# Backward pass of sliding-window attention: visits of four key blocks instead of steps of three, with the key-side slabs kept over two chunks

## The chip, the core and the metric

The kernel runs on one core of a Trainium2 chip. The metric is the device time of one execution in microseconds (us); less is better. Engines are named as in the profile: PE (TensorE matmul), PEld (its weight load), DVE (VectorE), ACT (ScalarE), POOL (GpSimd) and SP (SyncE, whose queue issues every DMA here; the profile calls the queue SPq). Each engine runs its own instructions in the order in which the kernel lists them.

## The reference

Four layers in a row, linear attention (A) and sliding-window softmax attention (B) in turn, each with a layer norm before and a residual around, and the gradients of the whole for a given output gradient. S = 2048 rows, D = 640, H = 32 heads of Dh = 20, window W = 256.

```python
def _B_ref(x, wqkv, wo):
    qkv = ((x @ wqkv).reshape(B, S, 3, H, Dh)).transpose(2, 0, 3, 1, 4)
    scores = einsum("bhqd,bhkd->bhqk", q, k) * (Dh ** -0.5)
    mask = (i - j >= 0) & (i - j < W)
    p = softmax(where(mask, scores, -1e9))
    o = einsum("bhqk,bhkd->bhqd", p, v)
    return o.transpose(0, 2, 1, 3).reshape(B, S, D) @ wo
x = x + A(layernorm(x));  x = x + B(layernorm(x))
x = x + A(layernorm(x));  x = x + B(layernorm(x))
out, vjp = jax.vjp(f, A_x, A_wqkv, A_wo, B_wqkv, B_wo);  grads = vjp(grad_out)
```

The change concerns the backward pass of the two B layers (layers 3 and 1), and the form in which the forward pass stores q, k and v for them.

## The kernel before

The execution has five parts in a row: the forward pass (to about 655 us of the span), the attention backward of layer 3 (its first score exponentials start at 654.7 us), the linear backward of layer 2, the attention backward of layer 1 (from 1255.2 us), and the linear backward of layer 0 with the products for the weight gradients.

The attention backward (`core`, L1191) cuts the 2048 rows into 16 query blocks of 128. A **chunk** is two query blocks, so there are 8 chunks for each layer. A query block sees up to three key blocks: its own, the one before and the one before that. Heads go in 8 groups g of four, and a head takes 32 rows of the PE array. One **step** (`core_steps`, L627) is one query block, one pair p of a group's heads, and its three key blocks: 2 heads x 3 blocks, 768 columns. That is 32 steps a chunk: 8 groups x 2 query blocks x 2 pairs.

`core_step` (L655) is a software pipeline written out by hand, with a fixed order on each engine. In step n:

- PE computes `dp` for step n-3 (two matmuls of 384 columns on 32 rows each) and then the scores `s` for step n (two more, on the other 64 rows). Both go to PSUM tiles of which there is only one each (`pS`, `pD`, two banks each).
- ACT takes the exponential, `e` (L677). DVE multiplies, `ds = dp * e` for step n-3 (L680). POOL masks two blocks of `e` (L689, L693).
- The transposed product `dsT` is needed as well. For 13 of 32 steps (the list `bd` of PLACES, used from the third chunk on) a DMA transposes it, issued on SP right after `ds`. For the other steps PE transposes step n-4 into a PSUM tile `flip` (L700), after some idle transposes that keep PE's clock up (`warm`, L173, numbers in `thin`), and ACT (L705) or DVE (L707) copies it out; `on_act` says which, by a count of both engines' loads.
- Then comes a "piece": work of other stages that is put into the step's slot by a list of places (`bf` for `plan_before`, which makes the next chunk's output gradients; `bh` for `plan_behind`, which takes an earlier chunk's dq, dk, dv through the projection, the layer norm and the next product).
- Last, `core_acc` (L713) sums dk, dv and dq of step n-7 (`lag` = 7) with 18 matmuls of 20 columns into two PSUM banks. After each group's four steps ACT and DVE take the sums out (L753 or L755, L757, L759).

The tags "flip" and "dense" share two PSUM banks (`ps2`). A quarter of a chunk (two groups, 8 steps) has one set of slabs: q, k, v transposed (`qT`, `kT`, `vT`) and q, k plain (`qs`, `ks`). `core_loads` (L1176) loads all five at once, one quarter ahead, with k and v for the four key blocks that the chunk sees; three sets are in use by turns. In the forward pass `qkv` (L493) stores q, k, v plain (`sv["s"]`, with v) and transposed (`sv["T"]`), one DMA each for a block of 128 rows.

Chunk 0 sees fewer key blocks (256 or 512 columns a step). Chunks 0 and 1 use no DMA transposes and have no work of `plan_behind`. Chunks 2 to 7 are called steady below.

Of the kernel before, what the change touches and what calls it, by code (L numbers as in the profile page):

```python
# [15 lines left out]
P = 128  # L16
# [30 lines left out]
    bf=[2.1, 3.1, 5.2, 14.9, 17.9, 6.2, 7.8, 10, 14.6, 28.3],  # L47
    bh=[13.1, 14.5, 15.5, 17.1, 17.5, 18, 20, 21.2, 25.7, 28.3, 30, 36, 19.1, 20.1, 21.8, 22.5, 23.3, 24.6, 25.2, 27.5, 30.5, 31.7, 33, 35, 41.5, 43, 2.2, 8.3, 9.5, 12, 18.9, 34.5],
    l2=[-10.4, -1.3, 0.6, 1.2, 1.9, 3.2, 4.6, 6.2, 7, 7.5, 5, 8, 8.3, 10.2, 11.8, 14, 14.4, 15.4, 16, 16.2, 18.7, -2.3, 4.4],
    n1=[9.7, 0.5, 3.3, 3.6, 5.3, 9, 3, 4.7, 5.4, 5.6, 24],  # L50
    xx=[1, 1, 0, 0, 0, 0, 1, 1, 0, 0, 0, 0, 0, 1, 0, 0, 1, 0, 0, 0, 0, 0, 0, 1, 0, 0, 1, 0, 0, 0, 1, 0],
    bd=[0, 0, 1, 0, 0, 0, 1, 0, 0, 0, 0, 0, 0, 1, 1, 0, 0, 1, 1, 0, 1, 0, 1, 0, 1, 0, 1, 1, 0, 1, 1, 0])


class Kern:
    def __init__(self, ctx, tc, x0, A_w, A_wo, B_w, B_wo, grad, outs):
# [27 lines left out]
        for l in (1, 3):  # L84
            self.sv[l] = {k: d(f"{k}{l}", [TT, P, 3, G * P]) for k in ("s", "T")}
# [20 lines left out]
    def dma(self, out, in_, transpose=False):  # L106
        with self.nc.allow_non_contiguous_dma(reason="tiled layouts"):
            return self.nc.sync.dma_start(out=out, in_=in_, transpose=transpose)  # L108

# [129 lines left out]
    def forward(self, st):  # L239
# [28 lines left out]
        st.ring, st.va, st.turn = [], [], 0  # L268
# [32 lines left out]
        def scores():  # L301
# [6 lines left out]
                 (B1 - 1, scores), (c3, lambda: self.close_outer(self.mz[2])),  # L308
# [27 lines left out]
        def before(a):  # L336
            if a == 0:
                first_.update(enumerate(self.slots(self.plan_before(st, 3, 0, st.core, ((1, 2, 3, 8, 10), (2, 4, 5, 10, 12))), 16)))
            if first_[a] is not None:
                first_[a]()  # L340
# [18 lines left out]
    def plan_scores(self, st, l, t, X):  # L359
# [37 lines left out]
        def values(g):  # L397
            self.b_pv(st, l, t, g, [home[g, i] for i in range(nb)], nb, [ring(k0 + i) for i in range(nb)], X[t]["ob"])
# [11 lines left out]
    def plan_ln(self, st, l, t, x, src, key, pool):  # L410
# [3 lines left out]
        def stats(c):  # L414
            if c == 0:
                x["bst"] = st.sm.tile([P, 2, 6], F32, name="bst")
            nc.vector.bn_stats(x["bst"][:, c, :], x[src][:, c * CW:(c + 1) * CW])

        def norm():
            mv = st.sm.tile([P, 2], F32, name="bmv")  # L420
# [13 lines left out]
    def plan_front(self, st, la, lb, t, x, x_in, Wo, W, Wq=None):  # L434
# [24 lines left out]
        def num(c):  # L459
            if c == 0:  # L460
                x["o"] = st.fb.tile([P, D], BF, name="o", bufs=2)
# [12 lines left out]
        def flip_o():  # L474
            self.dma(self.rows(self.o[la], t), x["o"])
# [17 lines left out]
        def qkv(j, c):  # L493
            ps = self.dense(st, x["hnT"], W, j * D + c * CW)
            dst = R["s"][:, j, c * HALF:(c + 1) * HALF, 0:DH]
            src = self.heads(ps[:, 0:CW])
# [6 lines left out]
            if (j, c) == (1, 1):  # L503
                self.dma(R["T"][:, 0:2].rearrange("p a g q -> p (a g) q"), R["s"][:, 0:2].rearrange("p a h d -> p (a h d)"), transpose=True)
            if (j, c) == (2, 1):
                self.dma(sv["s"][t], R["s"].rearrange("p a h d -> p a (h d)"))
                self.dma(R["T"][:, 2], R["s"][:, 2].rearrange("p h d -> p (h d)"), transpose=True)
                self.dma(sv["T"][t], R["T"].rearrange("p a g q -> p a (g q)"))
# [14 lines left out]
    def plan_rear(self, st, l, t, x, x_out, Wo, W):  # L523
# [3 lines left out]
        def flip_o():  # L527
            x["obT"] = self.flip(st.ps, st.fa, x["ob"], "obT", P, DT, P, nc.vector)
# [49 lines left out]
    def plan_feat(self, st, l, t, x, src, W):  # L578
# [8 lines left out]
        def feat_(nm, c, split=False):  # L587
            ps = self.dense(st, x["h2T"], W, {"pq": 0, "pk": D, "v": 2 * D}[nm] + c * CW)
            if nm == "v":
                vt = st.va[t % len(st.va)]  # L590
                nc.scalar.copy(vt[:, c * HALF:(c + 1) * HALF, 0:DH], self.heads(ps[:, 0:CW]))
# [7 lines left out]
            def close():  # L599
                part()  # L600
                if nm == "pk" and c == 1 and l == 2:
# [10 lines left out]
        def outer(c=None):  # L612
            a, b = x["pqk"][:, 1, :], st.va[t % len(st.va)].rearrange("p h d -> p (h d)")
            if c is None:
                if "og" not in x:
                    x["og"] = self.acc_outer(st, [(a, b)], t == 0)
                next(x["og"])
# [9 lines left out]
    def core_steps(self, st, l, S, c, qr, dq):  # L627
# [3 lines left out]
        for g in range(2 * qr, 2 * qr + 2):  # L631
            for bi in range(2):
                b = t0 + bi
                k0 = max(b - 2, 0)
                for p in range(2):
                    class U:
                        pass
                    u = U()
                    u.c, u.g, u.gi, u.b, u.bi, u.p, u.S, u.dq, u.t0, u.w0 = c, g, g - 2 * qr, b, bi, p, S, dq, t0, w0
                    u.nb = b - k0 + 1  # L640
                    u.kk = k0 - w0
                    u.cw = u.nb * P
                    u.by_dma = self.by_dma(32 * c + 4 * g + 2 * bi + p)
                    yield u

    @staticmethod
    def by_dma(n):

        return n >= 64 and PLACES["bd"][n % 32] == 1

    WARM = (6, 4)
    TAIL = 5
    FULL = 3600

    def core_step(self, st, l, u, piece, on_act, thin):  # L655
# [7 lines left out]
        d, f, a = back(3), back(4), back(st.lag)  # L663
        if d is not None:
            d.dp = st.pD.tile([P, 2, 512], F32, name="dp")
            for j in range(2):
                r0 = HP * (2 * d.p + j)
                self.mm(d.dp[:, j, 0:d.cw].rearrange("p (a b) -> p a b", a=d.nb), d.S["dT"][d.bi][r0:r0 + HP, d.g, :],
                        d.S["vT"][r0:r0 + HP, d.kk:d.kk + d.nb, d.gi, :], True, True, (r0, 0))
        if u is not None:  # L670
            s = st.pS.tile([P, 2, 512], F32, name="s")
            for j in range(2):
                r0 = HP * (2 * u.p + j)
# [786 lines left out]
```

## Time and profile before

| | |
|---|---|
| three runs | 2200.07, 2201.24, 2201.99 us; median 2201.24 |
| the profiled execution: its time, its span | 2199.58 us, 2197.9 us; granted PE clock 0.984 |
| DVE, ACT, POOL busy, share of the span | 63%, 61%, 49% |
| DMA moved | 453.26 MB, 81.2% of 16 engines' span |
| first exponential of layer 3's chunks 0 to 7 | 654.7, 699.3, 751.6, 807.1, 865.0, 920.6, 975.6, 1033.3 us |
| first exponential of layer 1's chunks 0 to 7 | 1255.2, 1297.5, 1349.8, 1404.7, 1460.9, 1516.8, 1571.8, 1629.9 us |
| slab loads, KB each (x count) | qT 128 (x64), kT 256 (x56), vT 256 (x56), qs 128 (x64), ks 256 (x56) |
| forward stores of q, k, v, KB each (x count) | plain 768 (x32), transposed 768 (x32) |

Differences of neighbouring entries in the two rows of first exponentials give the time of a chunk: 44.6, 52.3, 55.4, 57.9, 55.7, 54.9 and 57.7 us for layer 3's first seven. A view by window gives, for such a stretch, the busy time of each engine with its number of instructions. A view of the waits lists who waited for whom, with the sum, the number and the longest. "PE busy" counts a stretch in which matmuls are in flight; their ends are modelled.

### The profile page before, as it was taken

Reading aid. Unit: us, or ns where it says so; the run is one execution under the profiler, and the core shown is the slowest. Engines: PE = TensorE matmul, PEld = TensorE weight load, DVE = VectorE, ACT = ScalarE, POOL = GpSimd, SP = SyncE. Lnnn points to the kernel's source line nnn. Section 1 sums busy time; section 2 is a strip of 40 time slices with the busy share of each in tenths; the row PEclk is TensorE's granted clock in tenths of the full one; section 3 lists DMA queues with packets and bytes.
Section 4 is the critical chain, followed back from the end, with each engine's and each line's share of the span. In section 5 each row is a group of like instructions: output and inputs, shape, how many; then the busy total and the mean of one; then the engine's idle time right before and its main releaser. Section 6 shows DMA issues by size and latency. Waiting matters only on the chain. (4 is left out here: it accounts for less than half of the span.)

```text
span 2197.9 us, 74336 instructions
## 1 busy us (share of the span) xinstructions
PE 2041.3 (93%) x30981; PEld 1586.3 (72%) x30981; DVE 1390.2 (63%) x2840; ACT 1342.4 (61%) x2009; POOL 1083.0 (49%) x1887
## 2 busy tenths in 40 slices
PE   7989998899989999998879899999988899999999
PEld 5667776577767877777768687777776788888644
DVE  6788886888836887887748668888876233320000
ACT  5468886388876887887637677888876233330000
POOL 2046665166675577777534456777764312220000
PEclk9999999999999999999999999999999999999999
DMA  7498885799979499998799734999987999998650
GB/s 258 146 253 229 237 233 146 171 234 245 232 218 255 111 200 198 210 206 192 157 293 275 198 106 115 197 208 202 210 189 165 271 307 246 266 228 241 220 162 21
DMA packets 708193, 453.26 MB, mean 206 GB/s; under 512 B 419728, under 2 KB 684688, under 8 KB 707472
## 3 DMA queue, kind: packets, MB, share of 16 engines
q1 hardware_dynamic: 707856, 448.51, 81.2%
q8 instruction: 242, 3.96, 0.8%
q14 instruction: 95, 0.78, 0.1%
HBM read 213.09 MB, written 149.82 MB: 165 GB/s over the span
## 5 line engine op out<-in xcount | busy, mean ns | idle before, releaser
L680 DVE TENSOR_TENSOR ds<-dp,e 128x768 bf16<-128x768 f32 (+2 forms) x512 | 464.0, 906 | 173.8 <-PE s L138 55.6
L677 ACT ACTIVATE e<-s 128x768 bf16<-128x768 f32 (+2 forms) x512 | 395.7, 773 | 137.5 <-PE s L138 110.4
L383 ACT ACTIVATE eT<-sT 128x2048 bf16<-128x2048 f32 x180 | 338.0, 1878 | 89.0 <-PE sT L138 85.2
L138 PE MATMUL wg<-rhs,lhs 128*128 128x240 bf16 (+3 forms) x2880 | 372.2, 286 | 7.7 <-DMA lhs<-o 7.7
L138 PEld LDWEIGHTS <-lhs 128*128 128x128 bf16 x2880 | 262.1, 98 | 97.2 <-DMA lhs<-o 9.6
L689 POOL TENSOR_SCALAR_AFFINE_SELECT e<-e 128x256 bf16<-128x256 bf16 x512 | 207.2, 406 | 249.8 <-ACT e L677 246.9
L138 PEld LDWEIGHTS <-dqT 128*128 128x128 bf16 x1920 | 171.8, 98 | 62.2 <-issue 10.4
L391 POOL TENSOR_SCALAR_AFFINE_SELECT eT<-eT 128x512 bf16<-128x512 bf16 x256 | 165.5, 650 | 98.7 <-ACT eT L383 98.7
L138 PE MATMUL acc<-slabqs,ds 128*128 128x20 bf16 x2880 | 210.0, 172 | 1.4 <-ACT dq L759 0.5
L138 PE MATMUL dp<-slabvT,dT 32*128 32x384 bf16 (+2 forms) x1024 | 168.0, 320 | 44.3 <-DVE ds L680 39.6
L138 PE MATMUL acc<-ds,e 128*128 128x20 bf16 x2880 | 208.0, 171 | 0.0
L138 PEld LDWEIGHTS <-ds 128*128 128x128 bf16 x2880 | 187.9, 96 | 11.7 <-issue 3.5
L693 POOL TENSOR_SCALAR_AFFINE_SELECT e<-e 128x256 bf16<-128x256 bf16 x448 | 194.9, 435 | 0.0
L138 PEld LDWEIGHTS <-e 128*128 128x128 bf16 x2880 | 170.0, 96 | 10.6 <-issue 1.8
L1140 DVE CAST wr<-wg 128x240 bf16<-128x240 f32 (+3 forms) x54 | 24.4, 452 | 240.1 <-PE wg L138 228.8
L700 PE MATMUL flip<-ident,ds 128*128 128x128 bf16 x1944 | 169.7, 221 | 3.3 <-DVE ds L787 1.2
L138 PE MATMUL s<-slabkT,slabqT 32*128 32x384 bf16 (+2 forms) x1024 | 167.9, 323 | 4.1 <-ACT e L677 3.5
L1138 ACT CAST wr<-wg 128x240 bf16<-128x240 f32 (+3 forms) x36 | 14.3, 397 | 245.9 <-PE wg L138 241.3
L1033 POOL TENSOR_TENSOR dh<-dh,lg 128x640 f32<-128x640 f32 x32 | 46.0, 1437 | 238.1 <-DVE s L1030 235.1
L138 PE MATMUL dense<-WTA,dqT 128*128 128x320 bf16 x960 | 162.6, 301 | 0.6 <-DVE dqT L1007 0.3
L138 PE MATMUL dense<-WB,hnT 128*128 128x320 bf16 x960 | 160.1, 301 | 0.4 <-DVE s L500 0.3
L138 PE MATMUL acc<-slabks,dsT 128*128 128x20 bf16 x2880 | 147.3, 171 | 14.0 <-DMA dsT<-ds 13.0
(175 smaller groups left out, 4483.0 us busy)
## 6 DMA issues: line engine op xcount, KB each, us to landing
s<-s SPq DMA_DIRECT2D x32, 768.0 KB, 4.1
T<-T SPq DMA_DIRECT2D x32, 768.0 KB, 3.9
dqkv<-dq SPq DMA_DIRECT2D x16, 960.0 KB, 5.6
dqkv<-dqa SPq DMA_DIRECT2D x32, 480.0 KB, 5.1
rhs<-dqkv SPq DMA_DIRECT2D x32, 480.0 KB, 5.4
rhs<-dqkv SPq DMA_DIRECT2D x16, 960.0 KB, 6.5
slabkT<-T SPq DMA_DIRECT2D x56, 256.0 KB, 4.4
slabvT<-T SPq DMA_DIRECT2D x56, 256.0 KB, 3.9
```

The costliest lines, as they stand in the source:

```text
L138: return self.nc.tensor.matmul(out, lhsT=lhsT, rhs=rhs, start=start, stop=stop, skip_group_check=True, **kw)
L383: nc.scalar.activation(e, s, ACT.Exp)
L391: nc.gpsimd.affine_select(out=e, in_=e, compare_op=ALU.is_ge, fill=0.0, base=0, pattern=[[0, 4], [1, P]], channel_multiplier=-1)
L677: nc.scalar.activation(u.e[:, :, 0:u.cw], s[:, :, 0:u.cw], ACT.Exp)
L680: nc.vector.tensor_tensor(out=d.ds[:, :, 0:d.cw], in0=d.dp[:, :, 0:d.cw], in1=d.e[:, :, 0:d.cw], op=ALU.mult)
L689: nc.gpsimd.affine_select(out=dg, in_=dg, compare_op=ALU.is_ge, fill=0.0, base=0, pattern=[[0, 2], [-1, P]], channel_multiplier=1)
L693: nc.gpsimd.affine_select(out=fr, in_=fr, compare_op=ALU.is_ge, fill=0.0, base=-1, pattern=[[0, 2], [1, P]], channel_multiplier=-1)
L700: nc.tensor.transpose(ps[:, 3 * j + i, :], f.ds[:, j, i * P:(i + 1) * P], self.ident)
L1033: nc.gpsimd.tensor_tensor(out=x["dh"], in0=x["dh"], in1=L["g"][:, i, :], op=ALU.add)
L1138: nc.scalar.copy(o[:, 0:w], ps[:, 0:w])
L1140: nc.vector.tensor_copy(o[:, 0:w], ps[:, 0:w])
```

## The change

The unit of the pipeline becomes a **visit**: four (query block, key block) pairs times two heads, 1024 columns, two full banks. A quarter's two groups have 12 such block pairs for each head pair; they are cut into three visits, so a chunk has 24 visits instead of 32 steps. The same blocks are computed. A visit's blocks are not all of one query block: `s` and `dp` of a visit are issued as "runs" of neighbouring key blocks of one query block (three, two and three runs for the three visits), those of `dp` and of `s` in turn. `lag` is 6 visits. `dsT` has eight blocks; 11 of 24 visits have it transposed by DMA (`bd`). Which engine copies a `flip` and how many idle transposes go before it now comes from fixed lists (`xx`, `th`), in place of the counts. A visit has two places for pieces, before and after `core_acc`; `bf` and `bh` have new numbers, in units of a 32nd of a chunk as before. The sums are taken out after every three visits, for a head pair of two groups, with DVE's add in two halves. Masks at two places of a visit go in one POOL instruction of 512 columns.

The stored transposed q, k, v get a layout with the quarter outside, written by three DMAs in pieces of 512 bytes a row; v is no longer stored plain. A quarter's load is now one DMA for k and v transposed of the chunk's own two blocks, and one for q transposed; the plain k and q are loaded by two more, issued in the second visit of the quarter itself. The blocks of the chunk before are taken from its slabs, which are kept (seven `slabT`, six `slabks`). `B.sf` has one buffer instead of two. The rest are assertions, which issue nothing.

```diff
-    bf=[2.1, 3.1, 5.2, 14.9, 17.9, 6.2, 7.8, 10, 14.6, 28.3],
+    bf=[3, 4.5, 7.7, 8.8, 17.9, 7.2, 9.7, 10, 13.9, 28.1],
...
-    xx=[1, 1, 0, 0, 0, 0, 1, 1, 0, 0, 0, 0, 0, 1, 0, 0, 1, 0, 0, 0, 0, 0, 0, 1, 0, 0, 1, 0, 0, 0, 1, 0],
-    bd=[0, 0, 1, 0, 0, 0, 1, 0, 0, 0, 0, 0, 0, 1, 1, 0, 0, 1, 1, 0, 1, 0, 1, 0, 1, 0, 1, 1, 0, 1, 1, 0])
+    th=[0, 2, 0, 4, 1, 1, 0, 1, 1, 2, 0, 2, 0, 1, 0, 3, 5, 1, 2, 1, 3, 0, 3, 1],
+    xx=[1, 0, 1, 1, 0, 1, 1, 1, 1, 1, 1, 1, 0, 1, 0, 1, 0, 1, 1, 1, 1, 0, 0, 1],
+    bd=[0, 1, 0, 0, 0, 0, 0, 1, 0, 1, 1, 0, 1, 1, 1, 0, 0, 1, 1, 1, 0, 1, 0, 0])
...
-            self.sv[l] = {k: d(f"{k}{l}", [TT, P, 3, G * P]) for k in ("s", "T")}
+            self.sv[l] = dict(s=d(f"s{l}", [TT, P, 2, G * P]), T=d(f"T{l}", [TT, P, 4, 3, 2 * P]))
...
-                self.dma(sv["T"][t], R["T"].rearrange("p a g q -> p a (g q)"))
+                for j in range(3):
+                    self.dma(sv["T"][t][:, :, j], R["T"][:, j].rearrange("p (c g) q -> p c (g q)", c=4))
...
-    def core_steps(self, st, l, S, c, qr, dq):
+    def core_visits(self, st, l, S, c, qr, dq):
...
+        for p in range(2):
+            if c == 0:
+                order = [[(0, 0), (1, 0), (1, 1)]] * 2
+            else:
+                order = [[(0, 0), (0, 1), (1, 1), (0, 2), (1, 2), (1, 3)], [(0, 0), (0, 1), (0, 2), (1, 2), (1, 3), (1, 1)]]
+            units = [(gi, bi, kk) for gi in range(2) for bi, kk in order[gi]]
+            m = len(units) // 3
+            for v in range(3):
...
+                u.blocks = units[v * m:(v + 1) * m]
...
+                u.by_dma = self.by_dma(24 * c + 6 * qr + 3 * p + v)
...
-    WARM = (6, 4)
+    WARM = (8, 5)
...
+    def core_pairs(self, u, out, lhs, rhs):
+
+        def pair(run):
+            gi, bi, kk, j0, n = run
+            for j in range(2):
+                r0 = HP * (2 * u.p + j)
+                self.mm(out[:, j, j0 * P:(j0 + n) * P].rearrange("p (a b) -> p a b", a=n), lhs(gi, bi)[r0:r0 + HP],
+                        u.S[rhs](kk, n)[r0:r0 + HP, :, gi, :], True, True, (r0, 0))
+        return [(run[0], lambda run=run: pair(run)) for run in u.runs]
...
+            x, y = pairs
+            while x or y:
+                for z in (x, y):
+                    if z:
+                        z.pop(0)[1]()
...
-            u.e = st.pe.tile([P, 2, 3 * P], BF, name="e")
-            nc.scalar.activation(u.e[:, :, 0:u.cw], s[:, :, 0:u.cw], ACT.Exp)
+            w = u.m * P
+            u.e = st.pe.tile([P, 2, 4 * P], BF, name="e")
+            nc.scalar.activation(u.e[:, :, 0:w], s[:, :, 0:w], ACT.Exp)
...
+            d.ds = st.pd.tile([P, 2, 4 * P], BF, name="ds")
+            nc.vector.tensor_tensor(out=d.ds[:, :, 0:w], in0=d.dp[:, :, 0:w], in1=d.e[:, :, 0:w], op=ALU.mult)
+            d.dsT = st.pt.tile([P, 8, P], BF, name="dsT")
+            if d.by_dma:
                 self.dma(d.dsT, d.ds.rearrange("p j k -> p (j k)"), transpose=True)
...
-        if piece is not None:
-            piece()
+        if piece[0] is not None:
+            piece[0]()
         if a is not None:
             self.core_acc(st, l, a)
+        if piece[1] is not None:
+            piece[1]()
...
             if old is not None:
-                nc.vector.tensor_tensor(out=kv(old), in0=av(st.acc[0]),
-                                        in1=st.part[:, (G * c + g + 1) % (G + 1), :].rearrange("p (b w x) -> p b w x", b=2, w=2), op=ALU.add)
+                for b in range(2):
+                    nc.vector.tensor_tensor(out=cols(old, 1, 2)[:, b], in0=acc(st.acc[0])[:, b],
+                                            in1=acc(st.part[:, (n + 1) % (G + 1), :])[:, b], op=ALU.add)
...
-        st.lag = 7
+        st.lag = 6
...
+        new = dict(c=c, qr=qr, T=B.keep.tile([P, 2, 2, 2, P], BF, name="slabT", bufs=7))
+        old = B.kept[-4] if c else None
+        B.kept.append(new)
...
+        part(new["T"], "T", 1, 2)
+        part(q, "T", 0, 1)
...
+        def late():
+            new["s"] = B.keep.tile([P, 2, 1, 2, P], BF, name="slabks", bufs=6)
+            q = B.slab.tile([P, 2, 1, 2, P], BF, name="slabqs", bufs=2)
+            part(new["s"], "s", 1, 1)
+            part(q, "s", 0, 1)
...
+        nv = 24 * NC + st.lag
+        off = 32 * NC + 7
+        slots = self.slots([(a * 1.5, f) for a, f, *_ in plan if a * 0.75 < nv], 2 * nv)
+        slots = list(zip(slots[0::2], slots[1::2]))
...
+        thin = [PLACES["th"][n % 24] for n in range(nv)]
+        for n in range(48):
+            thin[n] = self.WARM[n // 24]
+        on_act = [PLACES["xx"][n % 24] for n in range(nv)]
```

## The prediction

> **What bounds the kernel now.** I read the page first. PE is busy for nearly the whole span:
>
> ```profile
> PE 2041.3 (93%) x30981; PEld 1586.3 (72%) x30981; DVE 1390.2 (63%) x2840; ACT 1342.4 (61%) x2009; POOL 1083.0 (49%) x1887
> ```
>
> The change lies in the two attention backwards, so the second view is the busy time by window, cut at the first exponential of layer 3's chunks (window; PE, PEld, DVE, ACT, POOL busy with instruction counts; PE clock, DMA share, GB/s). Chunks 1, 4 and 6:
>
> ```profile
> 699.33:751.63 52.30, 50.48 (x1012) 42.58 (x1012) 40.86 (x59) 43.10 (x68) 31.65 (x75) 1.00 0.56 151
> ...
> 864.98:920.63 55.65, 51.50 (x986) 41.14 (x984) 44.90 (x66) 44.96 (x76) 42.52 (x83) 1.00 1.07 209
> ...
> 975.56:1033.28 57.72, 51.55 (x986) 41.26 (x984) 44.91 (x66) 45.02 (x75) 41.97 (x83) 1.00 0.87 192
> ```
>
> In a steady chunk PE has 51.5 us of work; the rest, 4.2 or 6.2 us, is PE waiting. DVE and ACT are at 81%. So a chunk gets shorter only by PE work taken away or PE waits taken away. Third, the waits inside chunk 4 (total us, times, longest):
>
> ```profile
> PE dp L138 <- DVE ds L680: 2.8, 7, 0.9
> ...
> PE acc L138 <- DMA dsT<-ds: 0.8, 2, 0.5
> ```
>
> Two causes: `dp` waits until DVE has read the previous `dp` (about 2.9 us a steady chunk), and a DMA-transposed `dsT` comes late. For the latter the listing by tile has 13.0 us in 12 waits over both layers, 1.1 us a steady chunk; chunk 6 alone has 2.7. No PE row names a slab.
>
> Fourth, prices by shape (busy us, mean ns):
>
> ```profile
> L680 DVE TENSOR_TENSOR ds<-dp,e 128x768 bf16<-128x768 f32 x448 | 428.4, 956 | 147.4 <-PE s L138 51.9 <-ACT dsT L705 24.4 <-DMA dsT<-ds 15.3
> L677 ACT ACTIVATE e<-s 128x768 bf16<-128x768 f32 x448 | 364.2, 813 | 120.3 <-PE s L138 97.6 <-POOL e L689 11.1 <-POOL e L693 3.3
> L707 DVE COPY dsT<-flip 128x768 bf16<-128x768 bf16 x134 | 73.4, 548 | 0.0
> L812 ACT COPY dT<-flip 128x1024 bf16<-128x1024 bf16 x32 | 32.5, 1014 | 16.8 <-PE flip L811 16.8
> ```
>
> Fifth, PE in order of time, in a step, and in the forward scores (start us, us):
>
> ```profile
> 900.95 0.17 PE L138 MATMUL acc<-slabqs,ds 128*128 128x20 bf16 x1
> ...
> 901.48 0.33 PE L138 MATMUL dp<-slabvT,dT 32*128 32x384 bf16 x2
> ...
> 901.75 0.85 PE L138 MATMUL dense<-WTB,dqT 128*128 128x320 bf16 x5
> ...
> 905.11 0.51 PE L700 MATMUL flip<-ident,ds 128*128 128x128 bf16 x6
> 905.45 0.84 PE L138 MATMUL dense<-WTB,dqT 128*128 128x320 bf16 x5
> ```
>
> ```profile
> 501.85 0.29 PE L138 MATMUL sT<-T,T 32*128 32x128 bf16 x8
> ...
> 502.19 0.85 PE L138 MATMUL dense<-WB,hnT 128*128 128x320 bf16 x5
> ```
>
> Prices are distances between starts. 18 `acc` matmuls take 0.53 us (900.95 to 901.48) at 0.0256 each, so 0.07 is lost at a step's join. `dp` and `s` of a step, four matmuls on four row strips, take 0.27. A transpose takes 0.34/6 = 0.057. Sixteen forward score matmuls of 128 columns, four on the four strips at a time, take 0.34: 0.085 for four.
>
> **The change, part by part (a steady chunk).** PE:
>
> - Joins: 32 become 24, 8 x 0.07 = -0.6.
> - Transposes: 19 steps x 6 = 114 become 13 visits x 8 = 104, 10 x 0.057 = -0.6. Idle transposes: 16 in the trace of a steady chunk; in the new lists the entries of `th` on visits that flip by PE add up to 16. Nothing.
> - `s` and `dp`: 32 x 0.27 = 8.6 become, per three visits, four runs of one block and four of two, 32 of each a chunk. One block costs 0.085; two, by the line between 0.085 and 0.27, 0.178. Sum 8.4: -0.2. No row shows two blocks: if all blocks cost 0.085 it is 8.2 (-0.4), if two cost as much as three 11.4 (+2.8). I take the middle, since both neighbours are rows on four strips.
>
> The Trainium skill speaks against this part: "TensorE: Matmul & The Clock Gate", section "Wait — 56ns, not 53.3ns?", says that matmuls never start less than about 25 ns apart, however small. The forward row has 0.34/16 = 21 ns, so it disagrees a little; by the rule one block costs 0.100, the part +0.3 rather than -0.2, and the total would be 6 us higher, 2176. I keep the row.
>
> DVE: the rows of `ds` with 768, 512 and 256 columns (956, 691, 424 ns) give 1.04 ns a column, so 1222 for 1024. 24 x 1.222 + two copies at 0.68 + 16 half adds at 0.32 (half of the 485 row's columns at that slope) = 35.8, against 32 x 0.956 + 8 x 0.548 + 8 x 0.485 = 38.9: -3.1. A visit also has a pitch of about 54/24 = 2.25 us and a `ds` of 1.22, so 1.03 is left for DVE's other work (now 1.74 - 0.96 = 0.78), while a single long piece still takes 1.3. So the wait of `dp` shrinks. Between nothing and all of it (0 to -2.9) I take half: -1.4.
>
> ACT: `e` of 1024 columns, by the slope of 813, 602 and 385, is 1027; 24 x 1.027 + 11 copies x 1.014 = 35.8 against 32 x 0.813 + 11 x 0.801 = 34.8, +1.0, and 8 fewer instructions overlap their neighbours (by 0.07 us, from busy time against the sum of durations): +1.5. It stays below PE, at 46.5 of 54, hidden by PE's own work; but five visits in a row (6 to 10) flip with the copy on ACT, 2.1 us each with the sums taken out, close to the pitch. Between 0 and +1.5 I take +0.5.
>
> The late `dsT`. Before, from the end of `ds` to the first product that reads `dsT` there are about 7.1 us (four steps of 1.74, plus 0.27 + 0.35 + 0.69 + 0.31 of that step, less the 1.45 at which `ds` ends); landing takes this long:
>
> ```profile
> DMA to landing us min/median/max: 2.7/3.8/7.3
> ```
>
> After, there are three visits, 6.75 + 0.26 + 0.46 + 0.69 + 0.41 - 1.8 = 6.8 us, and eight blocks instead of six: a median between 3.8 and 3.8 x 8/6 = 5.1, a longest up to 9.7. Against that, slab traffic falls from 1024 to 640 KB a quarter in a stage where DMA is full (share 1.07). So between all gone (-1.1) and four more late ones of 1.1 us (+4.4) I take +0.5.
>
> POOL masks: 64 x 0.42 = 26.9 becomes 16 x 0.64 + 32 x 0.42 = 23.7; POOL at 76% with two steps to spare hides them. Fewer slab bytes are worth nothing by themselves: no PE wait names them, and the plain k and q loaded in the second visit have four visits (9 us) against 3.6 of landing.
>
> Steady chunk: -0.6 - 0.6 - 0.2 - 1.4 + 0.5 + 0.5 = -1.8; 12 of them, -21.6. Chunk 1 (no DMA transposes): joins -0.6, `s`/`dp` -0.2, idle transposes 128 to 120 -0.5, half of its 1.8 us of waits -0.9: -2.2, twice -4.4. Chunk 0: joins -0.6, idle transposes 28 x 6 to 20 x 8 -0.5, half of 3.0 us of waits -1.5: -2.6, twice -5.2. The drain, seven short steps or six, nothing.
>
> Forward: two more DMA issues a block, 64 in all at about 0.45 us of SP's time. They follow the store that already waits for the transposed v (SP waits 38.0 us in 28 times for `T`), so they sit in that wait, and PE is busy for 50.0 of 50 us there: nothing, and 29 us (64 x 0.45) if SP had no such slack. Packets of 512 bytes instead of 6 KB: the slab loads have 512-byte packets and move 256 KB in 4.4 us beside other traffic, the three stores are 256 KB each and nothing reads them for 100 us.
>
> Sum: -21.6 - 4.4 - 5.2 = -31.2. Against the profiled execution's own 2199.6 this is 2168.4; the median of the runs is 1.7 higher: **2170**.
>
> **Rivals.**
> 1. The waits go altogether: visits have room for every long piece and the freed DMA ends the late `dsT`. Steady -0.6 - 0.6 - 0.2 - 2.9 - 1.1 = -5.4, chunks 1 and 0 -3.1 and -4.1: -65 - 14 = -79, **2122**. For it: DVE falls to 42 of 51. Against: the longest piece is still longer than the room.
> 2. ACT sets the pace: its +1.5 lands on the path and `dp` waits as before. Steady -1.4 + 1.5 + 0.5 = +0.6, times 12 +7; chunks 1 and 0 gain 1.3 and 1.1 each: +2, **2203**, with 2188 if half of it holds. For it: 11 of 13 copies on ACT. Against: 86% busy is not full.
> 3. Slower: the bigger transposes miss their time. Four more late ones a chunk, 1.1 us each, in place of my +0.5: steady +2.1, times 12 +25, less 9.6: +16, **2217**. It decides from 37/12 = 3.1 us a chunk beyond today's 1.1. For it: median landing 5.1 of 6.8 us, and SP issues in order, so one blocked store delays all behind it. Against: 11 instead of 13, and less traffic.
> 4. The slabs do not do what they say (time from traffic): costed at nothing above, so nothing changes.
>
> **How the numbers follow.** Forecast (2150 to 2188) 0.53; rival 1 (below 2150) 0.15; rival 2 (2188 to 2205) 0.16, of which 0.10 is faster by over 0.2% and 0.06 within; rival 3 0.16. 0.2%, 4.4 us, is about what this measurement can tell from no change. Faster 0.53 + 0.15 + 0.10 = 0.78, same 0.06, slower 0.16. The range takes in half of rival 1 and the nearer half of rival 3: 2138 to 2212; the forecast's own is 2150 to 2188.
>
> **What would show it.** Steady chunks of 53 to 54.5 us with PE busy for about 50; `e` at 1.03, `ds` at 1.22 and the copy at 1.01 us; `dp` waiting for `ds` 1 to 2 us a chunk; `dsT` waits of 1 to 2; the forward's windows unchanged. I am wrong if PE busy does not fall, if `dsT` waits pass 3 us a chunk, or if the part before 655 us gets longer.

## The result, and the profile after

The changed kernel takes 2187.34 us (median of four runs, 2186.83 to 2187.87) beside 2200.65 for the kernel before on the same chip: ratio 0.9947, interval 0.993 to 0.9965. It is faster by 13 us where 31 were forecast.

The busy time by engine, from the page of the changed kernel:

```profile
PE 2023.2 (93%) x32575; PEld 1564.4 (72%) x32575; DVE 1338.7 (61%) x2710; ACT 1364.0 (62%) x1907; POOL 1040.7 (48%) x1663
```

PE is busy for 18.1 us less, DVE for 51.5 less, ACT for 21.6 more. PE also ran at a lower granted clock, 0.970 in this execution against 0.984 before (0.969 to 0.974 in all runs of the changed kernel, 0.975 to 0.987 in those of the kernel before), so its busy time understates the work that was taken away. Next, the same three chunks of layer 3 (1, 4 and 6) by window, columns as before (start:end, length, PE, PEld, DVE, ACT, POOL busy with counts, PE clock, DMA share, GB/s):

```profile
708.53:759.56 51.03, 48.69 (x1107) 41.69 (x1107) 37.28 (x48) 44.62 (x62) 29.68 (x58) 0.97 0.26 76
...
865.79:920.86 55.07, 49.70 (x1107) 39.31 (x1104) 41.45 (x61) 45.85 (x68) 39.07 (x66) 1.00 0.98 189
...
973.85:1030.44 56.59, 51.75 (x1101) 40.58 (x1099) 42.08 (x61) 46.20 (x69) 39.94 (x68) 0.94 0.82 170
```

In chunk 4 PE's busy time fell from 51.5 to 49.7; in chunk 6 it is 51.75 (51.55 before), but there the granted clock was 0.94 (1.00 before). The waits inside chunk 4 (total us, times, longest):

```profile
PE dp L142 <- DVE ds L723: 2.3, 4, 1.0
...
PE acc L142 <- DMA dsT<-ds: 1.3, 1, 1.3
```

Both waits of before are still there. The landing of the transposed blocks, now eight in each DMA instead of six, from the listing of `dsT`:

```profile
DMA to landing us min/median/max: 3.0/4.2/7.3
```

And the prices by shape:

```profile
L723 DVE TENSOR_TENSOR ds<-dp,e 128x1024 bf16<-128x1024 f32 x336 | 410.8, 1223 | 129.1 <-PE s L142 70.5 <-POOL e L738 17.5 <-ACT dT L871 14.7
L719 ACT ACTIVATE e<-s 128x1024 bf16<-128x1024 f32 x336 | 351.2, 1045 | 74.7 <-PE s L142 70.1 <-POOL e L738 3.0 <-POOL e L734 0.2
...
L750 ACT COPY dsT<-flip 128x1024 bf16<-128x1024 bf16 x166 | 172.0, 1036 | 7.4 <-PE flip L745 7.4
L752 DVE COPY dsT<-flip 128x1024 bf16<-128x1024 bf16 x38 | 25.9, 681 | 0.0
```

These are within 2.2% of the durations that were priced (1222, 1027, 1014 and 680 ns). So the rows were priced well, and the chunks of the visits gave about what was forecast. Cutting both profiled executions at the same places shows where the rest went. The marks are the first `e` of a chunk, the last `dq` that is taken out of a layer's sums, and ACT's first `lna` of the linear backward (us):

| stretch | before | after | difference | after, run again |
|---|---|---|---|---|
| to the first `e` of layer 3 (forward) | 654.7 | 664.2 | +9.5 | 666.2 |
| layer 3, chunks 0 to 6 | 378.5 | 366.2 | -12.3 | 368.1 |
| layer 3, chunk 7 and drain | 62.0 | 62.3 | +0.3 | 60.3 |
| handover to the linear backward | 57.9 | 63.1 | +5.2 | 62.8 |
| linear backward of layer 2 | 102.0 | 103.7 | +1.7 | 102.3 |
| layer 1, chunks 0 to 6 | 374.7 | 357.2 | -17.5 | 361.0 |
| layer 1, chunk 7 and drain | 65.3 | 60.5 | -4.8 | 59.1 |
| the rest | 502.7 | 508.3 | +5.6 | 505.4 |

The attention chunks gained 34.3 us (32.0 in the repeat), against 31.2 forecast. Outside them 22.0 were lost (19.3 in the repeat). The losses in the forward and the handover appear in both executions. The last row lies between 504.8 and 508.9 in every experiment below, with old and new parts alike, so nothing of it is put down to the change. Single stretches of equal code differ by up to 5 us between executions: layer 1's chunks 0 to 6 took 357.2, 361.0, 357.9 (e7) and 362.0 us (e4) with the same visits and loads.

Within the forward, the exponentials `eT` number 91 and 133 of 180 start at 414.3 and 532.5 us (415.2 and 532.5 before), the last at 659.7 (652.1 before): the loss arises after the 133rd, late in layer 3's forward, and none of it in layer 1's. Half of the 9.5 us is idle time of PE (51.9 us before, 56.8 after), half is longer busy time (602.8 and 607.5) at a granted clock of 0.97 in place of 0.98. In the window 440 to 650, before and after:

```profile
PE sT L138 <- DMA T<-s: 0.3, 1, 0.3
```

```profile
PE sT L142 <- DMA T<-s: 5.3, 7, 1.5
...
SPq L109 <- DMA T<-s: 43.6, 28, 4.3
```

PE now waits for the transposed q, k, v of a row block, and these waits name 5.3 of the 9.5 us (0.3 before). On SP's queue the stores wait for the same transposes (21.9 us in 13 waits before), which the prediction had named as the slack that hides them.

### The profile page after: what moved, and what is told of

Its sections match the earlier page's. It is cut to its first block, busy times and chain, and to the rows that moved or that the text cites. A ratio compares the mean times of both kernels' runs of the same rounds, so it can differ in the third digit from the quotient of the medians.

```text
span 2185.5 us, 76656 instructions
## 1 busy us (share of the span) xinstructions
PE 2023.2 (93%) x32575; PEld 1564.4 (72%) x32575; DVE 1338.7 (61%) x2710; ACT 1364.0 (62%) x1907; POOL 1040.7 (48%) x1663
## 5 line engine op out<-in xcount | busy, mean ns | idle before, releaser
L723 DVE TENSOR_TENSOR ds<-dp,e 128x1024 bf16<-128x1024 f32 (+1 forms) x384 | 443.9, 1156 | 166.0 <-PE s L142 80.5
L719 ACT ACTIVATE e<-s 128x1024 bf16<-128x1024 f32 (+1 forms) x384 | 380.1, 990 | 90.4 <-PE s L142 85.9
L738 POOL TENSOR_SCALAR_AFFINE_SELECT e<-e 128x256 bf16<-128x256 bf16 x512 | 201.6, 409 | 174.4 <-ACT e L719 143.8
L395 POOL TENSOR_SCALAR_AFFINE_SELECT eT<-eT 128x512 bf16<-128x512 bf16 x256 | 164.7, 647 | 102.3 <-ACT eT L387 102.3
L750 ACT COPY dsT<-flip 128x1024 bf16<-128x1024 bf16 (+1 forms) x200 | 192.2, 961 | 12.4 <-PE flip L745 11.2
L142 PE MATMUL acc<-slabqs,ds 128*128 128x20 bf16 x2880 | 194.3, 172 | 0.6 <-ACT dq L805 0.5
L142 PE MATMUL acc<-ds,e 128*128 128x20 bf16 x2880 | 192.2, 171 | 0.0
L142 PE MATMUL dp<-slabT,dT 32*128 32x128 bf16 (+1 forms) x1952 | 154.1, 246 | 38.4 <-DVE ds L723 32.1
L734 POOL TENSOR_SCALAR_AFFINE_SELECT e<-e 128x512 bf16<-128x512 bf16 x224 | 142.7, 637 | 55.6 <-ACT e L719 53.2
L142 PE MATMUL s<-slabT,slabqT 32*128 32x128 bf16 (+1 forms) x1952 | 148.4, 247 | 10.7 <-ACT e L719 5.2
L142 PE MATMUL dense<-WTB,dqT 128*128 128x320 bf16 x960 | 156.1, 301 | 1.1 <-DMA dqT<-dq 0.7
```

Of the source, the lines that this page charges most:

```text
L142: return self.nc.tensor.matmul(out, lhsT=lhsT, rhs=rhs, start=start, stop=stop, skip_group_check=True, **kw)
L395: nc.gpsimd.affine_select(out=e, in_=e, compare_op=ALU.is_ge, fill=0.0, base=0, pattern=[[0, 4], [1, P]], channel_multiplier=-1)
L719: nc.scalar.activation(u.e[:, :, 0:w], s[:, :, 0:w], ACT.Exp)
L723: nc.vector.tensor_tensor(out=d.ds[:, :, 0:w], in0=d.dp[:, :, 0:w], in1=d.e[:, :, 0:w], op=ALU.mult)
L734: nc.gpsimd.affine_select(out=v, in_=v, pattern=[[0, 4], [1 if far else -1, P]], **kw)
L738: nc.gpsimd.affine_select(out=v, in_=v, pattern=[[0, 2], [1 if far else -1, P]], **kw)
```

## The experiments

Every run's time in one table; a ratio is against runs of the kernel before on the same chip. The stretches are from one profiled execution each.

| run | median us | ratio, interval | forward | layer 3, 0-6 | handover | layer 1, 0-6 |
|---|---|---|---|---|---|---|
| e1_three_wide | 2186.51 | 0.9935 [0.9905, 0.9964] | 655.8 | 368.1 | 63.1 | 362.4 |
| e2_one_store | 2185.0 | 0.9921 [0.989, 0.9952] | 657.4 | 367.9 | 62.9 | 362.7 |
| e3_before_three_stores | 2226.93 | 1.0103 [1.006, 1.0145] | 682.9 | 375.3 | 58.8 | 372.6 |
| e4_old_tail | 2177.71 | 0.9884 [0.9851, 0.9916] | 664.4 | 363.9 | 57.6 | 362.0 |
| e6_two_small | 2197.85 (one) | | 667.0 | 368.7 | 63.1 | 364.4 |
| e7_plain_v | 2206.43 (one) | | 689.1 | 365.3 | 64.0 | 357.9 |
| g1_copies_dve | 2187.76 | 0.9943 [0.9921, 0.9964] | 664.8 | 368.4 | 62.8 | 356.7 |
| g2_full_slabs | 2199.61 | 0.9991 [0.9974, 1.0007] | 668.6 | 370.1 | 62.9 | 368.3 |
| g3_no_idle | 2186.72 | 0.9948 [0.9931, 0.9965] | 664.9 | 364.8 | 62.0 | 357.6 |
| e8_steps_kept | 2208.49 | 1.0041 [1.0025, 1.0058] | 652.1 | 381.2 | 57.9 | 376.2 |
| a0_after | 2184.44 | 0.9924 [0.9909, 0.9939] | 666.2 | 368.1 | 62.8 | 361.0 |
| b1_one_store_old_tail | 2174.49 | 0.9882 [0.9865, 0.9898] | 657.6 | 365.6 | 57.6 | 359.9 |

### The forward: how T is stored

e1: the changed kernel with the old layout of T, still in three stores a row block (pieces of 2 KB for each partition in place of four of 512 bytes). The slabs of k and v transposed are then loaded by two DMAs in place of one, also in e2, e6 and b1:

```diff
-T=d(f"T{l}", [TT, P, 4, 3, 2 * P])
+T=d(f"T{l}", [TT, P, 3, G * P])
...
-self.dma(sv["T"][t][:, :, j], R["T"][:, j].rearrange("p (c g) q -> p c (g q)", c=4))
+self.dma(sv["T"][t][:, j], R["T"][:, j].rearrange("p g q -> p (g q)"))
...
+for w in range(n):
+    src = sv[k][t0:t0 + 2, :, a + w, qr * 2 * P:(qr + 1) * 2 * P]
```

> The changed kernel with the transposed q, k, v in the old layout, but still stored by three DMAs (pieces of 2 KB instead of 512 bytes); k and v transposed are loaded by two DMAs a quarter. Measured so far: first score exponential of layer 3 at 654.7 us before, 664.2 after. Theory 1 (SP's queue: two stores that wait for the first transpose now stand ahead of the transpose of v, and the next tile's transposes stand behind the third store's wait): the time stays about 2187 and the first exponential at 662 to 666 us, with SP waiting some 30 us for transposes after 500 us. Rival (the 512-byte packets load the DMA engines): it goes back to 655 us and the total to about 2178.

e2: the same layout, one store a row block.

```diff
-for j in range(3):
-    self.dma(sv["T"][t][:, :, j], R["T"][:, j].rearrange("p (c g) q -> p c (g q)", c=4))
+self.dma(sv["T"][t], R["T"].rearrange("p a g q -> p a (g q)"))
```

> The same old layout, stored by one DMA as before the change; loads as in the run with three stores. Theory 1: first exponential back at 654 to 657 us, total about 2178. If the loss comes from the packets: the same. Rival (the loss comes from neither, but from the burst of slab loads at the end of the forward pass or the moved pieces before the first chunk): stays at 662 to 666 us and 2187.

e3: the kernel before with the new layout and three stores alone.

```diff
-self.dma(sv["T"][t], R["T"].rearrange("p a g q -> p a (g q)"))
+for j in range(3):
+    self.dma(sv["T"][t][:, :, j], R["T"][:, j].rearrange("p (c g) q -> p c (g q)", c=4))
```

> The kernel before with the new layout of the transposed q, k, v and its three stores, and nothing else of the change. Theory 1 and the packet rival: the forward pass alone takes the loss, first exponential at 660 to 665 instead of 654.7 us, total 2206 to 2210. Rival (the loss needs the rest of the change): first exponential at 655 us, total 2201.

The forward came back to 655.8 with three wide stores and 657.4 with one, and in the kernel before it grew by 28.2 us with the three narrow ones. That is far more than the 5 to 10 us that e3 was expected to lose. So the stores are the cause of the forward's loss, and their count alone is not. What differs between them is read on SP's queue. The listing of tile T, 440 to 640 us, gives the duration of an issue on SP (ns, least/median/longest): before, after, e1.

```profile
L108 SPq DMA_DIRECT2D T<-T x13: 319/319/712, 445.8 to 626.5; - x13
```

```profile
L109 SPq DMA_DIRECT2D T<-T x40: 528/534/654, 440.2 to 639.6; - x40
L109 SPq DMA_TRANSPOSE T<-s x26: 1237/1985/4217, 444.2 to 635.2; - x26
```

```profile
L109 SPq DMA_DIRECT2D T<-T x40: 319/320/677, 444.4 to 637.4; - x40
```

A store with 2 KB pieces holds SP for 0.32 us, one with 512-byte pieces for 0.53. A row block's stores held SP for 0.32 us before, for 1.6 after and for 0.96 in e1. Two readings were left: SP's time, or the small packets on the DMA engines. Two further kernels, each executed once, were made to tell them apart.

e6: e1 with two more tiny DMAs a row block (16 partitions of 256 bytes into a spare tensor that nothing reads), so but for 8 KB the bytes and packets are those of e1, and only SP has more to issue:

```diff
+for j in (0, 2):
+    self.dma(self.spare[t, j], R["T"][0:16, j, 0])
```

> The changed kernel with the three stores in pieces of 2 KB (first exponential of layer 3 measured at 655.8 us), plus two tiny DMAs a block of rows (16 partitions of 256 bytes) that wait for the same transposes. They bring SP's issue time per block back to that of three stores in 512-byte pieces (3 x 0.53 us against 3 x 0.32) with no load on the DMA engines. Theory now (512-byte packets on the DMA engines delay the transposes T): first exponential at 655 to 658 us. Rival (it was SP's time): 661 to 666 us.

e7: the changed kernel that stores the plain v again, as the kernel before did (768 KB in place of 512 KB a row block, read by nobody), with no further issue:

```diff
-s=d(f"s{l}", [TT, P, 2, G * P])
+s=d(f"s{l}", [TT, P, 3, G * P])
...
-self.dma(sv["s"][t], R["s"][:, 0:2].rearrange("p a h d -> p a (h d)"))
+self.dma(sv["s"][t], R["s"].rearrange("p a h d -> p a (h d)"))
```

> The changed kernel with v stored plain again in the forward pass, as before the change (768 instead of 512 KB a store, in the same single DMA, rows of 6 KB), never read. Theory (the DMA engines are the limit of the forward pass in the new layout): more bytes without more issues make the forward pass longer, first exponential at 670 to 680 instead of 664 us (the kernel before with the new layout, which stores v plain, had 682.9). Rival (only the order and time of SP's issues count): 664 to 667 us.

e6's forward took 667.0 us, 11.2 more than e1's. Issues on SP as above, then PE's wait in 100 to 668 us:

```profile
L110 SPq DMA_DIRECT2D spare<-T x26: 422/430/1396, 439.9 to 636.4; - x26
...
PE sT L143 <- DMA T<-s: 13.4, 9, 3.0
```

Two issues of 0.43 us a row block, which move 8 KB together, make a loss of this size by themselves: time on SP's in-order queue is enough, where the next block's transposes stand behind these DMAs, and smaller packets on the engines aren't needed for it. The sizes agree: over e1, a row block's stores hold SP 0.64 us longer in the changed kernel and 0.86 in e6, and the forward is 8.4 and 11.2 us longer (layer 3's forward has 16 row blocks). e7 lost even more, 689.1, while its other stretches are like the changed kernel's:

```profile
L109 SPq DMA_TRANSPOSE T<-s x24: 1962/2466/3719, 436.6 to 637.1; - x24
...
PE sT L142 <- DMA T<-s: 31.2, 20, 5.8
```

This is beyond both expectations, and nearer to the theory that the DMA engines are the limit (670 to 680) than to its rival (664 to 667). Against that theory, the DMA engines were less busy in the slower forwards: between 440 and 640 us their share was 0.93 before, 0.88 after the change and 0.83 in e7, at 235, 214 and 207 GB/s. With the longer store in the traffic and the narrow ones kept, the issue of a transpose holds SP for 2.47 us at the median, against 1.99 in the changed kernel (the kernel before, with the same bytes and a single store, has 2.52 and no loss). The reading that fits all of these is that a row block's place on SP is used up by both: by the narrow stores and by the bytes that lengthen the transposes' issue. It would also explain e3. For the bytes this is argued and not shown: no run added bytes and kept SP's time as it was. The change itself took 256 KB of v out of each block's stores, and this hid most of the cost of its narrow ones: with v stored, the forward is 28.2 us (e3) or 34.4 (e7) longer than before, without it 9.5.

Three stores and 64 more issues were costed at "nothing", and at 29 us without slack. The slack was there for layer 1 and partly there for layer 3.

e1 and e2 gave back 7 to 10 us of forward, yet their medians, 2186.51 and 2185.0, lie between the change's own 2184.44 and 2187.34. So undoing the loss of the forward in this way did not shorten the whole. Their `dsT` waits were 13.6 and 13.9 us, against 5.0 and 8.2, and their chunks 0 to 6 of layer 1 took 362.4 and 362.7 (357.2 and 361.0 in the changed kernel, but also 362.0 in e4, which loads as the change does). Their loads of k and v slabs have pieces of 512 bytes in place of 1 KB and are one more a quarter. That this is the reason was not isolated.

### The handover: pieces after the last visit

e4: the changed kernel, with the list `bh` of the kernel before (as `BH_TAIL`) for the pieces of the last two chunks.

```diff
-A = PLACES["bh"]
+A = BH_TAIL if c >= TT // 2 - 2 else PLACES["bh"]
```

> The changed kernel with the old places for the pieces behind the last two chunks (bh), all else as in the change. From the last sum taken out in layer 3 (1095.3 us before, 1092.7 after) to the first layer-norm piece of the linear backward (1153.2 and 1155.8) the change takes 5 us longer. Theory (the new places order the pieces after the last visit worse): that stretch goes from 63.1 back to about 58 us, total 2180 to 2184. Rival (PE's lower clock after a stall, or the end of the visits itself): 63 us and 2187.

The handover went from 63.1 to 57.6 us, the 57.9 of before, and the kernel to 2177.71. The windows of the handover, before, after and e4:

```profile
1095.31:1153.22 57.91, 45.19 (x420) 35.08 (x421) 25.01 (x58) 23.45 (x45) 20.94 (x17) 0.91 0.94 289
```

```profile
1092.71:1155.82 63.11, 49.23 (x420) 37.58 (x421) 24.63 (x58) 23.33 (x45) 21.00 (x17) 0.84 0.83 261
```

```profile
1087.61:1145.19 57.58, 44.87 (x418) 34.80 (x416) 24.82 (x58) 23.46 (x45) 20.98 (x17) 0.91 0.92 283
```

PE has the same 420 matmuls, which take 49.2 us in place of 45.2 at a granted clock of 0.84 in place of 0.91. Busy time times clock is 41 us in all three rows, so PE's 4 us more go with the lower clock. The new order on ACT, in order of time, is seen against e4's:

```profile
1108.57 0.92 ACT L966 ACTIVATE lna<-hnb,s,s 128x640 f32<-128x640 bf16 x1 [1.58 <-DVE s L959]
1109.40 0.67 ACT L169 COPY gT<-flip 128x640 bf16<-128x640 bf16 x1
```

```profile
1102.07 0.69 ACT L172 COPY gT<-flip 128x640 bf16<-128x640 bf16 x1 [0.49 <-PE flip L169]
1102.78 0.92 ACT L969 ACTIVATE lna<-hnb,s,s 128x640 f32<-128x640 bf16 x1
```

After the change `lna` stands ahead of the copy of `gT`, and that copy waits behind it, and behind the 1.58 us that `lna` itself waits. PE's next product waits for the copy (after, then e4):

```profile
1110.12 0.85 PE L142 MATMUL dense<-WoTA,gT 128*128 128x320 bf16 x5 [2.13 <-ACT gT L169]
1126.68 0.85 PE L142 MATMUL dense<-WoTA,gT 128*128 128x320 bf16 x5 [1.91 <-ACT gT L169]
```

```profile
1102.82 0.85 PE L145 MATMUL dense<-WoTA,gT 128*128 128x320 bf16 x5 [0.84 <-ACT gT L172]
1117.69 1.53 PE L145 MATMUL dense<-WoTA,gT 128*128 128x320 bf16 x10 [0.46 <-ACT gT L172]
```

That the new order makes these waits is shown by e4. The mean clock of 0.84 comes from stretches in which the clock is halved, within 2 us of the end of each of these two waits (after, by window, then e4's 25 us from its first such product on):

```profile
1111.20:1114.40 3.20, 3.20 (x17) 2.00 (x15) 0.76 (x2) 0.69 (x1) 0.24 (x1) 0.50 1.01 311
1128.30:1131.50 3.20, 3.20 (x16) 1.97 (x15) 0.72 (x2) 0.69 (x1) 0.75 (x1) 0.50 1.02 392
```

```profile
1102.80:1127.40 24.60, 16.98 (x142) 12.20 (x143) 9.69 (x22) 7.07 (x14) 16.94 (x14) 1.00 0.93 312
```

A third such stretch, behind a longer wait of PE that all three kernels have (3.5 to 3.8 us), lasts 13.5 us after the change (from 1135.1), and 10 us in the kernel before (from 1135.8) and in e4 (from 1127.6). So the waits of about 2 us and the halved clock go together in place and time; no run lowers the clock without the waits.

### The visits: slabs, ACT and the idle transposes

g1: three of the eleven copies of `dsT` that ACT makes in a chunk go to DVE (entries 7, 9 and 19 of `xx`).

```diff
-xx=[1, 0, 1, 1, 0, 1, 1, 1, 1, 1, 1, 1, 0, 1, 0, 1, 0, 1, 1, 1, 1, 0, 0, 1],
+xx=[1, 0, 1, 1, 0, 1, 1, 0, 1, 0, 1, 1, 0, 1, 0, 1, 0, 1, 1, 0, 1, 0, 0, 1],
```

> The changed kernel with three of the eleven copies of transposed tiles a chunk moved from ACT to DVE (visits 7, 9 and 19). Measured: ACT is busy 46 and DVE 41.5 of 53.8 us a steady chunk. Theory (PE's own work and the wait of dp for ds set the pace, ACT is hidden): 2185 to 2195, a little slower since DVE gets 2 us a chunk more and dp waits for DVE. Rival (ACT sets the pace, so that its extra load took the rest of the gain): steady chunks of 52 to 53 us, total 2170 to 2180.

2187.76 beside the 2184.44 of the changed kernel itself on the same chip: no gain, and `dp` waits 34.8 us for `ds` over the run (31.1 in a0_after). ACT does not set the pace.

g2: every quarter loads k and v of all four key blocks (1024 KB in place of 640) with the same number of DMAs, and nothing is kept.

```diff
-new = dict(c=c, qr=qr, T=B.keep.tile([P, 2, 2, 2, P], BF, name="slabT", bufs=7))
+new = dict(c=c, qr=qr, T=B.keep.tile([P, 4, 2, 2, P], BF, name="slabT", bufs=3))
...
-part(new["T"], "T", 1, 2)
+part(new["T"][:, 0:nk], "T", 1, 2, w0)
...
-i = w0 + kk - t0
-return new[k][:, i:i + n, a] if i >= 0 else old[k][:, 2 + i:2 + i + n, a]
+return new[k][:, kk:kk + n, a]
```

> The changed kernel with every quarter loading k and v of all four key blocks again, as before the change (1024 instead of 640 KB a quarter, in the same number of DMAs), so that nothing is kept over two chunks. Theory of the prediction (fewer slab bytes are worth nothing by themselves): 2185 to 2190. Rival (the smaller traffic is what cut the late DMA transposes, 13.0 us of PE waits before and 5.0 after): the waits for dsT go back to 10 us or more and the total to 2192 to 2200.

2199.61, 15 us above a0_after. PE's waits for a late `dsT` over the run, and the landing, of a0_after and then of g2:

```profile
PE acc L142 <- DMA dsT<-ds: 8.2, 12, 1.5
```

```profile
PE acc L142 <- DMA dsT<-ds: 15.5, 18, 1.8
...
DMA to landing us min/median/max: 3.0/4.6/9.1
```

The longest landing, 9.1 us, is near the 9.7 that the prediction feared for eight blocks. The named waits give 7.3 of the 15 us; the two columns of chunks 0 to 6 in the table give 9.3. With chunk 7 and the drains (62.6 and 60.8 in g2), the two attention backwards take 861.8 us in g2, 848.5 in a0_after and 880.5 before: without the kept slabs the visits still gain 18.7 us there, and the forward and the handover take it away again, so that the whole comes out level with the kernel before (0.9991).

e8: the kernel before with kept slabs alone (five tiles of a quarter's own two blocks; the products of a step that spans two chunks are split in two).

```diff
+    def parts(self, u):
+        m = u.t0 - u.w0 - u.kk
+        return [(0, m), (m, u.nb - m)] if 0 < m < u.nb else [(0, u.nb)]
...
-            for j in range(2):
+            for k0, n in self.parts(d):
+                for j in range(2):
...
+            new[nm] = B.slab.tile([P, 2, 2, P], BF, name="slab" + nm, bufs=dict(qT=2, qs=3).get(nm, 7))
```

> The kernel before, steps and store unchanged, with the key-side slabs kept over two chunks alone: a quarter loads k and v of its own two blocks only, and a step's score and dp products are split in two where they cross from the kept slab to the new one. Loading everything anew in the changed kernel cost 15 us (2199.6 against 2184.4). Theory (the smaller slab traffic is worth that by itself, through the late DMA transposes): the waits for dsT fall from 13.0 us to 8 or less and the total to 2185 to 2194. Rival of the prediction (fewer slab bytes are worth nothing by themselves; the steps are bound by PE and DVE): 2197 to 2203.

2208.49: no gain, 9 us worse. The `dsT` waits were 12.7 us, as before the change (13.0), with 640 KB a quarter in place of 1024; the chunks took 381.2 and 376.2 for 378.5 and 374.7, and the split products are extra work. So kept slabs by themselves, as e8 builds them, gave the steps nothing; what they would give without the split products was not measured. To the visits they are worth some 13 of the 32 us that the chunks gained.

g3: the idle transposes (`th`) left out of the steady chunks.

```diff
-th=[0, 2, 0, 4, 1, 1, 0, 1, 1, 2, 0, 2, 0, 1, 0, 3, 5, 1, 2, 1, 3, 0, 3, 1],
+th=[0] * 24,
```

> The changed kernel without the 16 idle transposes of a steady chunk (the list th all zero; chunks 0 and 1 keep theirs). If PE's own work sets the pace and the clock holds: 16 x 0.057 = 0.9 us a chunk less, 12 chunks, 11 us, 2173. If they fill time in which PE waits anyway: 2184 to 2188. If they hold the clock up: PE's granted clock in the visits falls below 0.97 and the total passes 2190.

2186.72, a ratio of 0.9948 beside the change's own 0.9947: no difference. The idle transposes fill time in which PE would wait. The granted clock of the profiled execution is 0.969 without them and 0.970 with them, so in the steady chunks they are not seen to keep PE's clock up.

### The change again, and the best version

> The changed kernel itself, for the comparison on one chip: 2187, ratio to the kernel before 0.993 to 0.997.

2184.44. b1 puts e2 and e4 together:

```diff
+self.dma(sv["T"][t], R["T"].rearrange("p a g q -> p a (g q)"))
...
+A = BH_TAIL if c >= TT // 2 - 2 else PLACES["bh"]
```

> The changed kernel with both losses undone: the transposed q, k, v in the old layout, stored by one DMA, and the old places for the pieces behind the last two chunks. If the two losses are independent: forward pass 655 to 658 us, layer 3's last chunk with the stretch to the linear backward 117 instead of 125 us, and a total some 14 to 18 us under the changed kernel on the same chip, about 2170. Rival (the core loses what the forward pass gains, because slab loads of 512-byte packets crowd the DMA transposes): no better than the run with the old places alone, 2178.

2174.49 (2174.02 to 2176.44), ratio to before 0.9882, and 10.0 below the change on the same chip: forward 657.6 (666.2) and handover 57.6 (62.8) have their times back, while the `dsT` waits rose from 8.2 to 12.8 us, which is part of why it is 10 and not the 14 to 18 expected. On that chip it is 25.9 us under the kernel before (2200.36), where the change alone is 15.9.

## Where the prediction was right, and why it was wrong

**Right: the attention chunks.** -31.2 was forecast for them, -34.3 came. The ten steady chunks 2 to 6 of both layers fell from 561.6 to 537.6 us, 2.4 each (forecast 1.8). PE's busy time fell 1.9 a chunk, where joins, transposes and the `s` and `dp` runs had been put at 1.4. Chunk 1 gave 1.3 and 2.0 (forecast 2.2), chunk 0 gave 0.3 and 2.2 (forecast 2.6). That the sum came within 3 us is in part luck: of its terms, PE's gave more and the wait of `dp` less than was put down, and the late `dsT` gained where a loss was put down.

The runs of one, two and one block, for which no row existed, are now in PE's order of time (one visit):

```profile
884.61 0.23 PE L142 MATMUL dp<-slabT,dT 32*128 32x128 bf16 x2
884.62 0.23 PE L142 MATMUL s<-slabT,slabqT 32*128 32x128 bf16 x2
884.68 0.27 PE L142 MATMUL dp<-slabT,dT 32*128 32x256 bf16 x2
884.69 0.27 PE L142 MATMUL s<-slabT,slabqT 32*128 32x256 bf16 x2
884.79 0.22 PE L142 MATMUL dp<-slabT,dT 32*128 32x128 bf16 x2
884.79 0.22 PE L142 MATMUL s<-slabT,slabqT 32*128 32x128 bf16 x2
884.95 0.23 PE L177 MATMUL flip<-ident 128*128 128x128 bf16 x1
```

All twelve take 0.34 us (884.61 to 884.95); 0.348 was the middle taken. The first four, two of `dp` and two of `s`, start within 0.01 us of each other, and the next four begin 0.07 us after them. The Trainium skill, "TensorE: Matmul & The Clock Gate", section "Wait — 56ns, not 53.3ns?", has about 25 ns as the least distance of two starts. The measurement decides against it for matmuls on different row strips.

**Right in sign, mis-sized: two waits.** "Between nothing and all of it I take half: -1.4" for `dp` behind `ds`: over both layers that wait went from 39.6 us in 95 times to 32.1 in 57, and in a steady chunk (2 to 6) from 2.8 to 2.2: 0.6 gained, not 1.4. The waits came more rarely, but the longest is 1.1 us as before. For the late `dsT` I took +0.5 a chunk; the waits went from 13.0 to 5.0 us (8.2 in the repeat), so the term has the other sign. The traffic that was saved weighed more than the larger transposes, as g2 shows by putting it back (15.5 us).

**Wrong: the forward.** The first step that failed is "so they sit in that wait, and PE is busy for 50.0 of 50 us there: nothing". I took one window of 50 us for the whole forward (between 600 and 650 us, near its end, PE was busy for 41.4 of 50 before the change), and the waits of SP for `T` as time that costs nothing. But SP issues in order. A store that waits, or that takes 0.53 us to issue instead of 0.32, holds back the transposes of the next row block, and late in layer 3's forward PE waits for these (7 times, 1.5 us at the longest). The size was +9.5 (+11.5 in the repeat). The prediction had named a longer stretch before 655 us as a sign of being wrong, and it came. e1, e2, e3 and e6 show the cause; how the bytes of v come into it (e7) is argued. The line on packet size looked at the DMA engines ("nothing reads them for 100 us"), and the cost of small pieces was on the issuing queue.

**Wrong: what was never costed.** This is the second step that failed, a term that the sum does not have. The prediction went through the visits and the drain, and not through the pieces that the new places push behind the last visit. "The drain, seven short steps or six, nothing" held (chunk 7 with its drain +0.3 and -4.8), but the 57.9 us that follow became 63.1. e4 shows that the new places alone did it: the 5.5 us are back, and its 2177.71 is 7 to 10 us below the changed kernel's two medians, on other chips; where the further 1 to 4 us lie is not shown. With both losses undone (b1) the change is worth 25.9 us, of the 31 that were forecast.

**Wrong as put, right in part: "Fewer slab bytes are worth nothing by themselves".** For the steps no gain was seen (e8, which also has extra products). For the visits the kept slabs carry 15 us of the whole: without them (g2) the changed kernel is level with the kernel before, 0.9991 with an interval that holds 1. Rival 3 had this mechanism, but even with the traffic back the `dsT` waits came to 15.5 us, far from the 50 (37 beyond today's 13.0) that it needed.

**The rivals.** Rival 1 (all waits gone, 2122) fell: PE is still idle for 3.9 us a steady chunk (4.4 before). Rival 2 (ACT sets the pace, 2203) fell in g1. Rival 3 (late transposes, 2217) fell: 5.0 us of waits where 37 beyond the 13.0 of before were its condition. Rival 4 does not hold: the traffic fell from 448.5 to 422.0 MB on the main queue.

What stays open: where e1 and e2 lose what they gain in the forward, and what the lower clock costs over the whole execution.

## What to carry to other kernels

Cost a layout's change at both ends and on the queue that issues it: a store with smaller pieces holds an in-order queue longer (0.53 us against 0.32 here), and what stands behind it there (here the next block's transposes) is what becomes late, not the store. When places in a schedule move, follow the pieces to the first one that lands after the loop, and look there at each engine's order. Cut the run into stretches before judging a stage: the stage forecast was right to 3 us here, and the total missed by more than half.

## What the runs showed of the hardware

- The issue of a DMA on SP took 0.32 us with pieces of 2 KB and 0.53 with pieces of 512 bytes; a DMA of 4 KB from 16 partitions still took 0.43. A DMA transpose held SP for 1.24 us at least, and its median there was 1.5 to 2.5 us, longer in the kernels that store more bytes beside it (1.99 in the changed kernel, 2.47 in e7, which adds the plain v alone).
- A transpose of eight 128x128 blocks landed in 4.2 us at the median, one of six in 3.8, so the two added blocks cost 0.4 us, and not the 1.3 of proportion.
- In one stretch with the same matmuls, PE was granted 0.84 of its clock with waits of about 2 us before products, and 0.91 with waits of 0.5 to 0.8. Over the traces of all runs here, 50 of 54 idle stretches of PE of 1.75 to 2.25 us that began at full clock were followed within 3.5 us of their end by a halved clock, and 137 of 608 of 0.75 to 1.25 us.
